# RWKV-6 and SiLU layer on one core: keys ahead of a weight sum, a tail ahead of its heads, one pair of copies on another engine, one unit's products in another order

## The chip, the core and the metric

The kernel runs on one core of a Trainium2 chip. The core has a matrix engine (TensorE, PE in the profile; its weight loads are shown apart as PEld), three engines for elementwise work (VectorE or DVE, ScalarE or ACT, GpSimd or POOL), a queue engine that issues most transfers (SyncE or SP), and 16 DMA engines. PSUM is the memory that PE writes; SBUF is the working memory. The metric is the device time of one execution in microseconds (us), as the median of three.

## What is computed

Two layers follow one another. The first is a linear recurrence over 768 time steps, for 4 batches and 8 heads of 48 channels:

```
for t in range(S):
    cur = u * k_t outer v_t
    y_t = r_t @ (state + cur)
    state = w_t[:, None] * state + k_t outer v_t
```

Its output is laid out as 3072 tokens by 384 channels, and goes through a layer of two matrix products with SiLU between them:

```
h = x @ w_in          # 384 x 2048
g = h / (1 + exp(-h))
out = g @ w_out       # 2048 x 384
```

All of it is in float32.

## The kernel before, in words

**Units.** The work is cut into 12 units of 128 time steps for two batches (6 stretches of time by 2 pairs of batches; unit i has number `i`, so the second unit is unit 1 and the third is unit 2). For a unit the recurrence is turned into products: `r` and `k` are scaled by growing products of `w`, level by level (`grow_queries` L626, `grow_keys` L632, levels 0 to 6), PE forms the scores of each level (`score_products` L691), VectorE writes them under a mask into the tile `score` (`keep_masked` L721), and PE multiplies scores and values (`x_products` L885 for units 0 and 1, `y_state` and `y_values` L840 to L876 later). The two layers behind it run one or two units late: while unit i is in its recurrence, unit i-1 is in its first product (`up` L1081 for units 0 to 2, `first_part` L1202 from unit 3 on) and unit i-2 in its second (`down` L1270 for unit 0, `quarter` L1312 after that).

**Order.** The order of all instructions is written out by hand. Each engine runs its own instructions in that order; semaphores join the engines. The early units are written out step by step (L1386 to L1442). From unit 3 on, `mix` (L967) gives groups of recurrence steps, and the loop at L1444 puts a counted number of the steps of `downs` (L1369, of unit i-2) and `ups` (L1353, of unit i-1) behind each group.

**Weights.** The 16 blocks of weights are rounded before use, each in three steps: `head_weight` (L221, two ScalarE instructions at L228 and L230), `tail_weight` (L232, one ScalarE instruction at L236 that writes the PSUM tile `p_w`), `join_weight` (L239, two VectorE instructions at L247 and L248, the second of which empties `p_w`), and `add_weight` (L256, one GpSimd addition at L260). `up(0, m)` needs block m. `join_weight` also issues the transfers of later blocks.

**Unit 1's start.** Its turned keys come from PE through four ScalarE copies (L386, L387). `odd_ones` (L659, ScalarE) and `start_keys` (L665) fill level 1's room of keys: with `own` true, two GpSimd products (L672) write the keys that the first scores of unit 1, `scores(1, 1)`, read; with `own` false two more change the rest in place. `turn_apart(0)` (L819) turns unit 0's keys back into the two PSUM banks `p_sc`, and `turn_k(0)` (L828) copies them to SBUF. `scores(1, 1)` writes the same two banks.

**Second product.** From unit 1 on `quarter` forms the second product by Winograd's seven products of half-size blocks. `sums` (L1295, VectorE, L1308) makes the four sums s1 to s4 of g, in four parts along the contraction. `quarter(i, which)` runs 16 matmuls (L1337) into one of three PSUM rooms: x, z, x, y, x, y, x for products 0 to 6. Products 2, 4 and 6 add onto what stands in x, and 5 onto y. ScalarE copies the room after 0, 2, 3 and 6 (L1342); VectorE adds after 1, 4 and 5 (L1345). Product 2 reads s2, product 3 reads s1, product 4 reads s3 and product 5 reads s4; `sums` makes them in the order s1, s3, s2, s4. For unit 2 and later, the rooms x, y, z are the banks `o0`, `o1`, `h1` that unit i+1's `first_part` uses next.

**First product.** From unit 3 on `first_part` forms h by 20 products of blocks (4x3 blocks of the weight by 3x2 of x, which the plain way takes 24 products), accumulated in four PSUM banks A to D (`ORDER` L1197), with copies, joins (L1220, VectorE) and SiLUs (L1217, ScalarE) between them. After product 1 VectorE runs two joins: one makes s32 from bank D, the other adds v22 onto bank A. Bank A is next written by product 11, three products later.

Of the kernel before, what the change touches and what calls it, by code (L numbers as in the profile page):

```python
# [15 lines left out]
ALU = mybir.AluOpType  # L16
# [22 lines left out]
def kernel(  # L39
# [11 lines left out]
    nc = tc.nc  # L51

    B, H, S, D = r.shape
# [5 lines left out]
    PD = 64  # L59
# [279 lines left out]
    for b in range(NB):  # L339
        for x in range(2):  # L340
            nc.vector.tensor_single_scalar(out=own_mask[:, b, :, x:x + 1], in_=first[0], scalar=tok[:, x, b:b + 1],
                                           op=ALU.is_equal)
# [485 lines left out]
    def turn_k(i):  # L828
        both_kq = pt.tile([128, NB, NP, 2 * PD], F32, name="kq", bufs=1)
        for b in range(NB):  # L830
            kq[i, b] = both_kq[:, b]
        for e, have in enumerate(apart[i]):
            nc.scalar.copy(out=both_kq[:, :, :, PD * e:PD * e + D], in_=have)

    p_yt, p_kv, yt = {}, {}, {}

# [124 lines left out]
    def both(fn, i, *args):  # L961
        return [(fn, i, b, *args) for b in range(NB)]
# [114 lines left out]
    FH, DH = FC // 2, DM // 2  # L1077
    NFAST = 3
# [106 lines left out]
    def first_layer(i, n):  # L1185

        place, first = ORDER[n]
        p = kept[place][:].rearrange("p (q t) -> p q t", q=4)
        left, right = left_of[n], right_of[i, n]
        for q in range(4):  # L1190
            for h in (0, PD):
                f = q * 128 + h
                nc.tensor.matmul(p[h:h + PD, q, :], lhsT=left[:, f:f + PD], rhs=right, start=first and q == 0, stop=q == 3,  # L1193
                                 skip_group_check=True)
# [7 lines left out]
    def first_part(i, n):  # L1202

        first_layer(i, n)
        pa, pb, pc, pd = (kept[x][:].rearrange("p (q t) -> p q t", q=4) for x in (A_AT, B_AT, C_AT, D_AT))

        def g(f, t):
            key = (i, PARTS[f][0], t - 1, PARTS[f][1])
            if key not in gt:
                gt[key] = pt.tile([128, 4, L], F32, name="gt", bufs=FC // 2)  # L1210
            return gt[key]

        def copy(out, in_):
            nc.scalar.copy(out=out, in_=in_)

        def silu(f, t, have):
            nc.scalar.activation(out=g(f, t), in_=have, func=AF.Silu)  # L1217

        def join(out, one, two, op):
            nc.vector.tensor_tensor(out=out, in0=one, in1=two, op=op)  # L1220

        u11, s32, s42, v22, w21 = (3, 1), (3, 2), (4, 2), (2, 2), (4, 1)
        if n == 20:
            copy(pb, pa)
        elif n == 18:
            copy(g(*u11), pc)
        elif n == 14:
            copy(g(*s32), pd)
        elif n == 13:
            join(pd, g(*u11), pa, ALU.subtract)  # L1230
        elif n == 15:
            silu(1, 1, pc)
        elif n == 4:
            copy(pc, pd)
        elif n == 7:
            nc.scalar.activation(out=g(*s42), in_=pb, func=AF.Copy, scale=-1.0)
            join(pb, pb, g(*s32), ALU.add)
        elif n == 19:
            join(g(*s42), g(*s42), pa, ALU.add)
        elif n == 16:  # L1240
            copy(g(*v22), pc)
        elif n == 1:
            join(g(*s32), g(*s32), pd, ALU.subtract)
            silu(3, 2, g(*s32))
            join(pa, pa, g(*v22), ALU.add)
        elif n == 9:
            silu(2, 2, pc)
        elif n == 11:
            copy(g(*w21), pa)
            join(pc, pb, g(*u11), ALU.subtract)  # L1250
            join(pb, pb, g(*w21), ALU.subtract)
        elif n == 6:
            silu(1, 2, pd)
        elif n == 10:
            join(pd, g(*s42), pb, ALU.add)
            silu(4, 1, pb)
        elif n == 5:
            silu(2, 1, pa)
        elif n == 8:
            silu(3, 1, pc)  # L1260
        elif n == 17:
            silu(4, 2, pd)
# [47 lines left out]
    ob, partial, sum_of = {}, {}, {}  # L1310

    def quarter(i, which):  # L1312

        n, b0 = units[i]

        def g(b, half):
            if i >= NFAST:
                return lambda f: gt[i, half, b, f // 4][:, f % 4, :]
            return lambda f: gt[i, (f + half * FH) // 2][:, f % 2, b * L:(b + 1) * L]

        def s(x):
            return lambda f: quarters[:, x, f, :]

        left, right = ((g(0, 0), b11), (g(0, 1), b21), (s(1), t2), (s(0), t1), (s(2), t3), (s(3), b22), (g(1, 1), b12))[which]
        if which == 0:
            ob[i] = [out_room(b) for b in range(NB)]
            partial[i] = pt.tile([128, 4, DH], F32, name="partial", bufs=1)
        place = "xzxyxyx"[which]
        if which in (0, 1, 3):
            if i < NFAST - 1:  # L1330
                pool, tag = (ps, "p_h") if place == "z" else (second[0], "p_o")
                sum_of[i, place] = pool.tile([128, DH], F32, name=tag, bufs=2)
            else:
                sum_of[i, place] = bank("p_sc", DH) if i == len(units) - 1 and which == 0 else kept[{"x": "o0", "y": "o1", "z": "h1"}[place]][:, 0:DH]
        p = sum_of[i, place]
        for f in range(FH):
            nc.tensor.matmul(p, lhsT=left(f), rhs=right[:, f, :], start=which in (0, 1, 3) and f == 0, stop=f == FH - 1,  # L1337
                             skip_group_check=True)
        c11, c12, c21, c22 = (ob[i][x][:, y * DH:(y + 1) * DH] for x in range(2) for y in range(2))
        u1, u2, u5 = (partial[i][:, x, :] for x in range(3))  # L1340
        if which in (0, 2, 3, 6):
            nc.scalar.copy(out={0: u1, 2: u2, 3: u5, 6: c21}[which], in_=p)  # L1342
        else:
            to, known = {1: (c11, u1), 4: (c22, u5), 5: (c12, u2)}[which]
            nc.vector.tensor_tensor(out=to, in0=p, in1=known, op=ALU.add)  # L1345
        final = i == len(units) - 1
        if which >= 5 or final and which in (1, 4):
            b = 1 if which in (4, 6) else 0
            row0 = (b0 + b) * S + n * L
            columns = slice(0, DM) if not final else slice(0, DH) if which in (1, 6) else slice(DH, DM)  # L1350
            nc.sync.dma_start(out=out[row0:row0 + L, columns], in_=ob[i][b][:, columns])
# [15 lines left out]
        return steps  # L1367

    def downs(i):  # L1369
        return [[(quarter, i, x)] for x in range(7)]  # L1370

    def do(*steps):
        for fn, *args in steps:
# [21 lines left out]
    for l in range(1, NL):  # L1395
# [1 line left out]

    do((bonus, 1, 0), (bonus, 1, 1), (product, 1, 0), (bonus, 1, 2), *both(x_products, 0), (join_weight, 0), (add_weight,),
       (x_copy, 0, 0), (tail_weight, 1), (x_copy, 0, 1), (turn_apart, 0), (turn_in, 1, 1, "k"), *both(turn, 1, "k"), (join_weight, 1),
       (odd_ones, 1), (add_weight,), (start_keys, 1, nc.gpsimd, True), (head_weight, 2), (grow_queries, 1, 0), (tail_weight, 2),  # L1400
       (up, 0, 0), (turn_k, 0), (join_weight, 2), *blocks[4:8],
       (start_keys, 1, nc.gpsimd, False), (add_weight,), (tail_weight, 3), (odd_keys, 1, 1), (head_weight, 3), (grow_keys, 1, 1),
       (scores, 1, 1, (join_weight, 3)), (add_weight,), (up, 0, 1), (tail_weight, 4), (grow_keys, 1, 2), (head_weight, 4),
# [92 lines left out]
```

## Time and profile before

| what | value |
|---|---|
| median of 3 executions | 567.58 us (567.09 to 568.59) |
| the profiled execution, its own time | 567.68 us |
| its span in the trace | 565.9 us, so 1.8 us lie around it |
| busy share of the span | PE 98%, PEld 92%, VectorE 84%, GpSimd 70%, ScalarE 48% |
| mean granted clock of PE | 0.997 |

The span runs from the first to the last instruction of the program. Busy time of PE counts overlapping pipeline time of matmuls, so 98% hides short waits; they show in the waits of PE and of its weight loads, and in the timeline. "x12" in a row is a count of instructions, the first number the start in us from the span's start, the second the length, and a note in brackets the idle time before it with what ended that idle time.

Where the stages lie: unit 1's recurrence begins near 31 us and ends near 66 us; unit 2's seven products of `quarter` run from 168.29 to 187.5 us, while unit 4's recurrence starts and unit 3's `first_part` follows from 188.81 us. Units 4 to 11 then repeat with about 42 us each.

### The profile page before, as it was taken

The page shows a single profiled execution, that of the slowest core. Times are in us where ns is not written, and L with a number is a line of the kernel's source. Part 1 is how long each engine was busy: PE and PEld are TensorE (multiplying, and loading weights), DVE is VectorE, ACT ScalarE, POOL GpSimd, SP SyncE. Part 2 cuts the span into 40 slices and gives each one's busy share as a digit, 9 for nine tenths or more (in the row PEclk, how much of TensorE's full clock was granted, in tenths as well). Part 3 has the DMA queues.
Part 4 walks back from the last instruction along what each step waited for, and adds up shares of the span by engine and source line. Part 5 has one row for each costly group of instructions (what it writes and reads, how often), then busy time and mean ns, then how long its engine had stood idle before and what let it go on. Part 6 is the DMA issues. An engine that isn't in the chain of part 4 may idle for free.

```text
span 565.9 us, 18889 instructions
## 1 busy us (share of the span) xinstructions
PE 556.3 (98%) x7782; PEld 518.0 (92%) x7782; DVE 477.0 (84%) x744; ACT 274.0 (48%) x619; POOL 397.4 (70%) x448
## 2 busy tenths in 40 slices
PE   8989999999999999999999999999999999999997
PEld 8768776699889999999999999999999999999997
DVE  7979788998999999999889989989989989882250
ACT  5679696362361373373374274274274272371330
POOL 6998988627779998969796696696696696700000
PEclk9999999999999999999999999999999999999999
DMA  9956866345445365265565554565555462102000
GB/s 223 312 109 196 208 218 125 48 67 111 108 74 98 73 112 95 57 130 96 102 105 96 109 93 88 108 97 94 111 90 94 105 99 61 38 4 57 29 9 21
DMA packets 206485, 57.59 MB, mean 102 GB/s; under 512 B 186048, under 2 KB 198208, under 8 KB 206400
## 3 DMA queue, kind: packets, MB, share of 16 engines
q1 hardware_dynamic: 203712, 54.23, 46.8%
q10 hardware_dynamic: 2688, 2.16, 1.6%
q8 instruction: 61, 1.00, 0.8%
q14 instruction: 24, 0.20, 0.1%
HBM read 47.14 MB, written 9.18 MB: 100 GB/s over the span
## 4 chain that ended last, share of the span: by engine, by line
PE 71%; DVE 11%; DMA 5%; POOL 5%; issue 3%; SPq 3%; ACT 0%; DVEq 0%; POOLq 0%
PE p_o L1337 24%; PE p_o L1193 14%; PE p_h L1193 9%; PE p_h L1086 5%; PE p_m L1275 4%; PE p_h L1337 4%; PE p_sc L706 3%; DVE temps L1308 2%; PE p_sc L1337 2%; PE p_m L870 2%; DVE tr L629 2%; DVE score L724 2%; PE p_m L849 1%; POOL tk L647 1%; DMA tokens_w<-in_w_dram 1%
## 5 line engine op out<-in xcount | busy, mean ns | idle before, releaser
L647 POOL TENSOR_TENSOR tk<-tk,tw 128x256 f32<-128x256 f32 x112 | 92.4, 845 | 5.1 <-PE p_sc L706 1.5
L1337 PE MATMUL p_o<-own,temps 128*128 128x192 f32 x496 | 82.9, 326 | 0.7 <-DVE temps L1308 0.7
L1337 PEld LDWEIGHTS p_o<-own,temps 128*128 128x128 f32 x496 | 80.8, 190 | 1.0 <-DVE temps L1308 0.9
L1193 PE MATMUL p_o<-xt,w_in_sb 128*64 128x128 f32 x1152 | 72.1, 273 | 0.0
L416 POOL TENSOR_TENSOR tw<-tw 128x256 f32<-128x256 f32 (+6 forms) x71 | 42.3, 595 | 37.5 <-DVE tw L366 34.0
L1086 PE MATMUL p_h<-xt,w_in_sb 128*128 128x256 f32 x288 | 67.8, 391 | 0.7 <-POOL w_in_sb L260 0.7
L1193 PEld LDWEIGHTS p_o<-xt,w_in_sb 128*64 128x64 f32 x1152 | 64.7, 137 | 0.1
L1086 PEld LDWEIGHTS p_h<-xt,w_in_sb 128*128 128x128 f32 x288 | 54.7, 194 | 9.4 <-POOL w_in_sb L260 1.1
L498 POOL TENSOR_TENSOR ruk<-tokens_rk 128x384 f32<-128x384 f32 x48 | 54.2, 1148 | 9.4 <-DMA tokens_rk<-in_k_dram 9.4
L1337 PE MATMUL p_o<-w_out_sb,gt 128*128 128x192 f32 x308 | 54.5, 330 | 0.4 <-DVE ob L1345 0.3
L629 DVE TENSOR_TENSOR tr<-tr,tw 128x512 f32<-128x512 f32 x57 | 51.0, 895 | 1.1 <-PE p_m L706 0.4
L1337 PEld LDWEIGHTS p_o<-w_out_sb,gt 128*128 128x128 f32 x308 | 50.0, 190 | 1.6 <-DVE ob L1345 1.0
L1308 DVE TENSOR_TENSOR temps<-gt 128x512 f32<-128x512 f32 (+1 forms) x48 | 43.7, 947 | 0.0
L656 POOL TENSOR_TENSOR tk<-tk,tw 128x256 f32<-128x256 f32 x32 | 25.1, 815 | 26.5 <-DVE tk L366 26.5
L1342 ACT COPY partial<-p_o 128x192 f32<-128x192 f32 x31 | 9.9, 319 | 67.3 <-PE p_o L1337 59.7
L617 ACT COPY tk<-tk 128x256 f32<-128x256 f32 x52 | 20.9, 401 | 38.2 <-POOL tk L647 27.4
L1217 ACT ACTIVATE gt<-p_o 128x512 f32<-128x512 f32 x45 | 26.0, 601 | 25.0 <-PE p_o L1193 25.0
L1337 PE MATMUL p_o<-w_out_sb,temps 128*128 128x192 f32 x176 | 30.5, 327 | 0.1
L724 DVE COPY_PREDICATED score<-mask,p_sc 128x512 f32<-128x512 int8 x38 | 28.4, 804 | 1.4 <-PE p_sc L706 1.3
L1337 PEld LDWEIGHTS p_o<-w_out_sb,temps 128*128 128x128 f32 x176 | 28.8, 190 | 0.4 <-ACT partial L1342 0.4
L1337 PE MATMUL p_h<-w_out_sb,gt 128*128 128x192 f32 x168 | 29.1, 326 | 0.0
L498 POOL TENSOR_TENSOR spare<-tokens_rk 128x384 f32<-128x384 f32 x24 | 28.4, 1197 | 0.6
(255 smaller groups left out, 1313.4 us busy)
## 6 DMA issues: line engine op xcount, KB each, us to landing
w_out_sb<-in_moe_w_in_dram SPq DMA_DIRECT2D x6, 768.0 KB, 7.2
turned<-yt SPq DMA_DIRECT2D x18, 192.0 KB, 2.6
xt<-turned SPq DMA_DIRECT2D x9, 384.0 KB, 3.4
w_out_sb<-in_moe_w_out_dram SPq DMA_DIRECT2D x4, 768.0 KB, 7.0
own<-in_moe_w_out_dram SPq DMA_DIRECT2D x4, 768.0 KB, 4.4
tokens_w<-in_w_dram SPq DMA_DIRECT2D x8, 384.0 KB, 4.4
tokens_rk<-in_r_dram SPq DMA_DIRECT2D x7, 384.0 KB, 4.3
tokens_rk<-in_k_dram SPq DMA_DIRECT2D x7, 384.0 KB, 5.9
```

The source lines that it names most:

```text
L416: engine.tensor_tensor(out=up, in0=t[:, :, 0::2], in1=t[:, :, 1::2], op=ALU.mult)
L498: mul = lambda out, one, two: nc.gpsimd.tensor_tensor(out=out, in0=one, in1=two, op=ALU.mult)
L629: nc.vector.tensor_tensor(out=odd, in0=odd, in1=tw[i][l][:, :, 0::2][:, :, :, None].to_broadcast([128, Q, L >> (l + 1), c]), op=ALU.mult)
L647: nc.gpsimd.tensor_tensor(out=out, in0=have, in1=odd_products(i, l, b, *blocks), op=ALU.mult)
L656: nc.gpsimd.tensor_tensor(out=have, in0=have, in1=odd_products(i, l, b, [2, NP * ni]), op=ALU.mult)
L724: nc.vector.copy_predicated(out=dst, mask=masks[l][:, :, None].to_broadcast([128, NB, NP, ni, c]), data=sc[e].rearrange("p (b q) (i c) -> ...
L1086: nc.tensor.matmul(p_h[:, a, :], lhsT=w_in_sb[:, c, f * 128:(f + 1) * 128], rhs=xt[i][:, c, :], start=(a == 0 and c == 0), stop=(a == 1 an ...
L1193: nc.tensor.matmul(p[h:h + PD, q, :], lhsT=left[:, f:f + PD], rhs=right, start=first and q == 0, stop=q == 3, skip_group_check=True)
L1217: nc.scalar.activation(out=g(f, t), in_=have, func=AF.Silu)
L1275: nc.tensor.matmul(po[i, b], lhsT=gt[i, f // 2][:, f % 2, b * L:(b + 1) * L], rhs=w_out_sb[:, f, :], start=(f == 0), stop=(f == FC - 1))
L1308: nc.vector.tensor_tensor(out=out, in0=one, in1=two, op=op)
L1337: nc.tensor.matmul(p, lhsT=left(f), rhs=right[:, f, :], start=which in (0, 1, 3) and f == 0, stop=f == FH - 1, skip_group_check=True)
```

## The change

It touches five places. Nothing of the arithmetic changes but the place and order of some additions.

- `turn_k` of unit 0: its two copies out of PSUM run on VectorE and no longer on ScalarE.
- `first_part`, product 1: the join that adds v22 onto bank A stands ahead of the join for s32 and the SiLU behind it (all units from 3 on).
- `quarter` of unit 2 (`i == NFAST - 1`): product 6 starts afresh in room z. For that, ScalarE also copies room x after product 4 (to a fourth part of `partial`, u3), and VectorE adds u3 to product 6's copy: one more instruction on each.
- `downs` of unit 2: the products run in the order 0, 1, 3, 2, 5, 4, 6.
- The order written out for unit 1's start: the two own-key products stand ahead of the addition of weight block 1 on GpSimd, and the tail of block 2 ahead of its two heads on ScalarE.

```diff
@@ turn_k
         for e, have in enumerate(apart[i]):
-            nc.scalar.copy(out=both_kq[:, :, :, PD * e:PD * e + D], in_=have)
+            (nc.scalar.copy if i else nc.vector.tensor_copy)(out=both_kq[:, :, :, PD * e:PD * e + D], in_=have)
@@ first_part
         elif n == 1:
+            join(pa, pa, g(*v22), ALU.add)
             join(g(*s32), g(*s32), pd, ALU.subtract)
             silu(3, 2, g(*s32))
-            join(pa, pa, g(*v22), ALU.add)
@@ quarter
-        place = "xzxyxyx"[which]
-        if which in (0, 1, 3):
+        apart_6 = i == NFAST - 1
+        place = ("xzxyxyz" if apart_6 else "xzxyxyx")[which]
+        fresh = (0, 1, 3, 6) if apart_6 else (0, 1, 3)
+        if which in fresh:
...
-            nc.tensor.matmul(p, lhsT=left(f), rhs=right[:, f, :], start=which in (0, 1, 3) and f == 0, stop=f == FH - 1,
+            nc.tensor.matmul(p, lhsT=left(f), rhs=right[:, f, :], start=which in fresh and f == 0, stop=f == FH - 1,
                              skip_group_check=True)
...
-        u1, u2, u5 = (partial[i][:, x, :] for x in range(3))
-        if which in (0, 2, 3, 6):
-            nc.scalar.copy(out={0: u1, 2: u2, 3: u5, 6: c21}[which], in_=p)
-        else:
-            to, known = {1: (c11, u1), 4: (c22, u5), 5: (c12, u2)}[which]
-            nc.vector.tensor_tensor(out=to, in0=p, in1=known, op=ALU.add)
+        u1, u2, u5, u3 = (partial[i][:, x, :] for x in range(4))
+        if which in (0, 2, 3) or which == 6 or which == 4 and apart_6:
+            nc.scalar.copy(out={0: u1, 2: u2, 3: u5, 4: u3, 6: c21}[which], in_=p)
+        if which in (1, 4, 5) or which == 6 and apart_6:
+            to, known = {1: (c11, u1), 4: (c22, u5), 5: (c12, u2), 6: (c21, u3)}[which]
+            nc.vector.tensor_tensor(out=to, in0=to if which == 6 else p, in1=known, op=ALU.add)
@@ downs
-        return [[(quarter, i, x)] for x in range(7)]
+        return [[(quarter, i, x)] for x in ((0, 1, 3, 2, 5, 4, 6) if i == NFAST - 1 else range(7))]
@@ the order of unit 1's start
-       (odd_ones, 1), (add_weight,), (start_keys, 1, nc.gpsimd, True), (head_weight, 2), (grow_queries, 1, 0), (tail_weight, 2),
+       (odd_ones, 1), (start_keys, 1, nc.gpsimd, True), (add_weight,), (tail_weight, 2), (head_weight, 2), (grow_queries, 1, 0),
        (up, 0, 0), (turn_k, 0), (join_weight, 2), *blocks[4:8],
```

## The prediction

> **What bounds the kernel now.** I read the waits of PE and of its weight loads first, because PE is busy 98% of the span: a change can gain only where PE waits, runs at a lower clock, or has another chain beside it that is as long.
>
> ```profile
> PE p_sc L706 <- POOL tk L672: 1.6, 1, 1.6
> ...
> PE p_o L1337 <- DVE temps L1308: 0.7, 1, 0.7
> ```
>
> ```profile
> PEld p_o L1337 <- DVE temps L1308: 0.9, 1, 0.9
> ...
> PEld p_h L1193 <- DVE p_h L1220: 0.8, 2, 0.4
> ```
>
> The columns are total us, times, longest. The change aims at these: the first scores of unit 1 wait 1.6 us for the own keys (L672), one product of unit 2 waits 0.9 us for a sum, and product 11 of `first_part` waits twice, 0.4 us each, for the join on bank A. From 31 us on no other single wait of either is longer than 0.9 us. Next, the table by windows, for the clock (the number behind the five busy times):
>
> ```profile
> 12.50:15.90 3.40, 2.34 (x26) 1.76 (x24) 3.29 (x6) 0.45 (x2) 2.49 (x4) 1.00 1.13 211
> ...
> 36.40:39.80 3.40, 1.94 (x37) 1.66 (x38) 2.76 (x3) 2.57 (x6) 2.74 (x5) 1.00 0.41 51
> 39.80:43.20 3.40, 3.40 (x10) 2.66 (x9) 3.30 (x4) 2.50 (x5) 3.05 (x4) 0.50 0.84 242
> ```
>
> The stretch that holds the 1.58 us wait has PE busy for 1.94 of 3.40 us (57%), and the next runs at clock 0.50: `up(0, 1)`'s 12 matmuls take 4.47 us and not 2.86. A stretch at 2.34 (69%) was not followed by a lower clock. The timeline from 33 to 45 us shows who made PE wait:
>
> ```profile
> 33.52 0.69 DVE L629 TENSOR_TENSOR tr<-tr,tw 128x512 f32<-128x512 f32 x1
> ...
> 33.68 2.20 POOL L260 TENSOR_TENSOR w_in_sb<-temps 128x768 uint32<-128x768 uint32 x1 [0.35 <-DVE temps L248]
> ...
> 35.85 2.53 POOL L672 TENSOR_TENSOR tk<-tk,tw 128x128 f32<-128x128 f32 x4
> 35.99 0.85 ACT L236 ACTIVATE p_w<-w_out_sb 128x768 f32<-128x768 uint16 x1
> ...
> 36.87 0.96 DVE L247 SCALAR_TENSOR_TENSOR p_w<-w_out_sb,p_w 128x768 uint32<-128x768 uint32 x1 [2.67 <-ACT p_w L236]
> ...
> 43.34 0.60 ACT L1095 ACTIVATE own<-p_h 128x512 f32<-128x512 f32 x1 [0.62 <-PE p_h L1086]
> ...
> 44.74 0.96 DVE L247 SCALAR_TENSOR_TENSOR p_w<-own,p_w 128x768 uint32<-128x768 uint32 x1 [0.78 <-ACT p_w L236]
> ```
>
> The own keys stand behind block 1's addition (33.68 to 35.88), and VectorE idles 2.67 us for block 2's tail. From 44.74 on VectorE has no idle over 0.14 us until 66 us, and GpSimd, behind it, ends block 7's addition at 63.03; `up(0, 7)` starts at 63.08. So past 44 us this chain, not PE alone, sets when PE reaches 63 us. After that PE runs through to 141 us. The chain of waits around unit 2's products is:
>
> ```profile
> 150.90 7.14 DMA tokens_w<-in_w_dram
> ...
> 166.04 1.84 DMA raw<-in_r_dram
> 167.90 1.30 DVE tk L366 x2
> ...
> 174.70 1.73 DVE temps L1308 x3
> 176.43 0.04 issue
> 176.47 11.32 PE p_o L1337 x68
> ```
>
> It leads from PE at 141 us over VectorE's reductions and SP into transfers, to VectorE, and back to PE. From 188 us a second such loop (PE, VectorE, block-sum transfers, VectorE, PE) runs to 272 us; behind it PE has no waits of size to the end.
>
> **Part 1, unit 1's start (order and `turn_k`).** I replay it from the rows.
> - Own keys: the turned keys are done at 33.51 (last L387), GpSimd is free at 33.33. Two products by 0.66 us. They now stand beside `grow_queries` (33.52 to 34.21); in unit 2 an L672 beside an L629 took 1.15 and its neighbours 0.67, so 0.47 more. End: 33.5 + 1.32 + 0.47 = 35.3 (before 37.13).
> - Copies of `turn_k` on VectorE: two by 0.56 (VectorE's copy of 128x384 out of PSUM, L905), from 34.2 to 35.3, inside the 2.67 us idle time. They free the `p_sc` banks; ScalarE did so at 38.10. Without that idle time they would cost 1.1 us. VectorE's PSUM copies at L940 (two by 0.55) stood beside an L260 of 1.82 us, so I charge GpSimd nothing for them.
> - Scores: PE is free at 36.2 and starts them there and not at 37.82: 1.6 us less.
> - Block 1's addition: 35.3 + 1.83 (an L260 that no L629 overlaps) = 37.1, 1.25 us later than before. `up(0, 1)` waits for it and starts at 37.15 (before 38.78). PE's wait shrinks to about 0.35 us, the stretch is over 80% busy, so by the rows the clock stays at 1.00.
> - Tail 2 follows `odd_ones` on ScalarE: 34.2 to 35.1 (before 36.84). Join 2: 35.3 to 37.3 (before 38.90). The heads end at 37.0, before block 2's addition needs them. That addition stands behind the two other key products: 37.1 + 1.3 + 1.83 = 40.2 (before 40.88).
> - From there the chain: level 1's two key products 1.45 (41.7), ScalarE's copy 0.42, SiLU 0.60, tail 4 0.87, so join 4 starts at 43.4 to 43.5 and not at 44.74. That is 1.25 us less. If the own keys meet less of `grow_queries` than I charged, 1.65. If they must also wait for `odd_ones` (34.25), 0.9. The three key products that wait for ScalarE do so for three different instructions, of which `odd_ones` would be the last, so I take 1.4.
>
> The rest of the early stage hangs on VectorE and moves with it. SP gets no new transfer; block 8's, issued in join 2, stands behind SP's own queue until 40.03 as before. So **PE passes 63 us 1.4 us earlier**, not 1.6 plus the 1.7 us that half clock cost: those are beside the chain.
>
> The Trainium skill, "SBUF — State Buffer", section "Who interferes with whom", speaks against this reorder: a VectorE instruction with two SBUF inputs and a GpSimd instruction that reads SBUF lock each other out, and the later one fully waits. By it the own keys would lose the whole 0.66 us left of `grow_queries` and not 0.47, and the sum would be 0.2 us smaller. The row (1.15 against 0.67) shows less, and I use it.
>
> **Part 2, unit 2's products.** Product 2 stood 0.95 us for the last part of s2, done at 176.43. In the new order product 3 is there, and reads s1, done by 175.3 (first of the L1308 at 174.70); its last quarter is due at 175.5, so no stall. Product 2 then needs s2 at 178.1, products 5 and 4 need s4 and s3, done by 176.88. ScalarE's copies (0.32) between products into the same room have a product between them. PE gains 0.92 us up to the scores at 187.72; their second half needs `prepare` (L785, done 186.99), which is early enough. Product 6 in z needs bank `h1` emptied (the add at 180.85) and must itself be copied before product 20: the scores between (0.96 us) cover that copy (0.32); without them it would cost 0.5 us. Room x is now freed by product 4's add, which stands where product 5's stood (189.67), for product 14 that would start at 189.65: 0.1 us. What follows:
>
> ```profile
> 192.69 0.70 DVE L1220 TENSOR_TENSOR p_o<-gt,p_h 128x512 f32<-128x512 f32 x1 [0.95 <-PE p_h L1193]
> ```
>
> This join opens the second loop. It waits 0.95 us for PE, VectorE being free at 191.74. The new add of u3 (0.35, as L1345; no row shows it with both inputs in SBUF, between nothing and L1308's 0.43 for 256 columns) pushes that to 192.1. So the loop opens **0.6 us earlier**; bounds 0 and 0.92.
>
> **Part 3, the join on bank A.** It may save the two waits (0.44 at 200.2, 0.39 at 244.0). Both lie inside the second loop, where PE waits again for VectorE (0.56 at 228.3, 0.44 at 271.6), so I take 0; bounds 0 and 0.8. The s32 join moves back by 0.7 us; product 3 needs its bank 2.6 us after product 1.
>
> **Sum.** 1.4 + 0.6 + 0 = 2.0 us off the profiled execution's 567.68 (span 565.9 and 1.8 around it): 565.7; this execution stood 0.1 above the median of 567.58, so **565.6 us** as a median. The bounds (0.9 + 0 to 1.65 + 0.92 + 0.8) give 564.2 to 566.7.
>
> **Rivals.**
> - *PE is the bound throughout*: the waits and the half clock all count: 1.6 + 1.7 + 0.9 = 4.2, 563.4 us. For it: PE runs without gaps from 38.8 to 62.9. Against: additions end just ahead of `up` (54.26 for 54.50, 63.03 for 63.08).
>   The Trainium skill, "TensorE: Matmul & The Clock Gate", "What's actually happening", has the clock fall only after at least one idle window of some 3.4 us; by that rule a 1.58 us wait didn't cause it and its end doesn't cure it, and this rival falls to 565.1. Here the fall followed a stretch that was 57% busy.
> - *Only one part arrives*: block 1's later addition holds the early chain, or the second loop is opened by GpSimd and not by this join: 566.2 (part 1 alone) to 567.0 (part 2 alone).
> - *A strip lands late, and it ends slower*: at 166.04 a strip of `raw` took 1.84 us to land and released VectorE's turn of k. Strips take 1.7 to 6.6 us. If the earlier PE work moves this one among other transfers and it takes 6.6, the loop loses 4.8: 570.4 us. It decides from a landing 2 us later than now. Against: all that feeds SP's queue there starts from VectorE at 147.5 and moves along.
>
> **Chances.** About 0.3% (1.7 us) is what a measurement of this kernel can tell from no change, so the line to faster is 565.9. The forecast has 0.60, of which three quarters lie under that line; PE throughout 0.15; one part alone 0.12; the late strip 0.13. Faster 0.45 + 0.15 = 0.60, same 0.15 + 0.12 = 0.27, slower 0.13. The range, 563.3 to 567.4, leaves out the late strip and the edges.
>
> **What would show it.** Right: L672 starts near 33.5 and ends near 35.3; no wait of PE on it; clock 1.00 from 39.8 to 43.2; join 4 near 43.4; `up(0, 7)` near 61.7; unit 2's products without a gap; the L1220 of 192.69 near 190.7. Wrong: half clock stays or appears elsewhere; join 4 moves but `up(0, 7)` doesn't; the `raw` strip or the block sums land at their old times.

## The result, and the profile after

| | before | after |
|---|---|---|
| median | 567.14 us (566.55 to 568.59, 11 runs) | 566.15 us (565.31 to 567.39, 11 runs) |
| profiled execution: time, span | 567.68, 565.9 us | 566.43, 564.6 us |
| mean granted clock in it | 0.997 | 1.0 |

The ratio of after to before is **0.9976 (95% interval 0.9967 to 0.9986)**, 1.4 us less (the two medians, taken by themselves, differ by 1.0 us). The gain is clear of zero, but it is under the 0.3% at which the prediction drew the line to "faster"; it had given that side of the line 0.60. Run again beside other kernels, the changed kernel gave 0.9982 (0.9969 to 0.9995). The forecast was 2.0 us.

**Unit 1's start came as forecast.** The timeline of the changed kernel from 33 to 45 us (start us, us, engine, line, operation):

```profile
33.34 1.75 POOL L672 TENSOR_TENSOR tk<-tk,tw 128x128 f32<-128x128 f32 x2
...
33.57 1.00 DVE L629 TENSOR_TENSOR tr<-tr,tw 128x512 f32<-128x512 f32 x1
...
34.48 1.01 DVE L833 COPY kq<-p_sc 128x384 f32<-128x384 f32 x2
...
36.23 0.70 PE L706 MATMUL p_sc<-tr,tk 48*64 48x64 f32 x32
...
43.06 0.96 DVE L247 SCALAR_TENSOR_TENSOR p_w<-own,p_w 128x768 uint32<-128x768 uint32 x1 [0.61 <-ACT p_w L236]
```

The own keys end at 35.09, the copies of `turn_k` at 35.49, the scores start at 36.23 without a wait, and join 4 starts at 43.06, 1.68 us earlier than before. The same two stretches of the table by windows (the number behind the five busy times is the clock):

```profile
36.40:39.80 3.40, 3.39 (x44) 2.59 (x40) 3.33 (x4) 3.32 (x6) 3.40 (x4) 1.00 0.42 51
39.80:43.20 3.40, 3.21 (x41) 2.62 (x44) 2.69 (x5) 2.51 (x5) 3.40 (x5) 1.00 0.51 99
```

PE is busy through the first and keeps its full clock in the second. What PE waits for in the early stage now are the weights' additions, as these lines of the waits of PE's weight loads and of PE show (total us, times, longest):

```profile
PEld p_h L1086 <- POOL w_in_sb L260: 3.0, 6, 0.9
...
PE p_h L1086 <- POOL w_in_sb L260: 1.5, 3, 0.7
```

So the chain of heads, tails, joins and additions sets the pace there, as the prediction had it. `up(0, 7)` starts at 61.55 and not 63.08. Set against the first `up` of unit 0, which stood 0.05 us later in this execution, PE has gained **1.58 us** at 63 us.

**Unit 2's products did not.** The gap at 176 us is gone: at 190 us PE is 2.52 us ahead of before, 0.96 more than at 174. Then the timeline from 187 us shows this:

```profile
188.07 0.89 DVE L1347 TENSOR_TENSOR ob<-ob,partial 128x192 f32<-128x192 f32 x1
188.70 2.09 POOL L498 TENSOR_TENSOR ruk<-tokens_rk 128x384 f32<-128x384 f32 x2
...
190.94 0.69 DVE L1220 TENSOR_TENSOR p_o<-gt,p_h 128x512 f32<-128x512 f32 x1
...
197.88 1.09 PE L1193 MATMUL p_o<-xt,w_in_sb 128*64 128x128 f32 x16 [0.73 <-POOL w_in_sb L1132]
```

The new addition of u3 took 0.89 us and not 0.35. The join L1220 does start 1.75 us earlier and no longer waits for PE. But PE then waits at product 9 for GpSimd's weight sum q9, 0.73 us for the product and 0.97 for its weight load. PE is 1.50 us ahead at 205, 1.12 at 210, and 1.25 from 275 us to the end: all that the new order of products had won is gone within 15 us, and some of part 1's gain with it. The chain of waits of the changed kernel says who holds PE there:

```profile
164.42 1.93 DMA raw<-in_r_dram
166.36 0.72 DVE tk L366
...
168.98 1.42 POOL w_in_sb L1132
...
188.74 2.05 POOL ruk L498 x2
190.79 2.48 POOL w_in_sb L1132 x2
...
193.34 2.97 POOL w_in_sb L1132 x2
196.53 1.26 issue
197.79 1.67 POOL tk L647 x2
```

From 167 to 199 us it hardly leaves GpSimd, which has no gap over 0.1 us there; it starts from the strip of `raw` that lands at 166.35. In the kernel before, the chain there went through PE's products. GpSimd's queue from 167 to 190 us moved by 1.55 us, as the strip's landing did (1.53), and not by PE's 2.5.

### The profile page after: what moved, and what is told of

Same layout as the page of the kernel before. It is cut to its first block, busy times and chain, and to the rows that moved or that the text cites. A ratio compares the mean times of both kernels' runs of the same rounds, so it can differ in the third digit from the quotient of the medians.

```text
span 564.6 us, 18890 instructions
## 1 busy us (share of the span) xinstructions
PE 555.2 (98%) x7782; PEld 516.8 (92%) x7782; DVE 477.3 (85%) x747; ACT 272.0 (48%) x618; POOL 396.2 (70%) x448
## 4 chain that ended last, share of the span: by engine, by line
PE 68%; POOL 12%; DVE 8%; DMA 4%; issue 3%; SPq 3%; ACT 1%; DVEq 0%; POOLq 0%
PE p_o L1339 22%; PE p_o L1193 13%; PE p_h L1193 9%; PE p_h L1086 4%; PE p_m L1275 4%; PE p_h L1339 4%; POOL tk L647 2%; PE p_sc L706 2%; PE p_sc L1339 2%; SPq L127 2%; POOL ruk L498 2%; PE p_m L870 2%; POOL tw L416 2%; POOL w_in_sb L1132 2%; DVE tr L629 2%
## 5 line engine op out<-in xcount | busy, mean ns | idle before, releaser
L647 POOL TENSOR_TENSOR tk<-tk,tw 128x256 f32<-128x256 f32 x112 | 88.6, 811 | 5.1 <-PE p_sc L706 1.5
L416 POOL TENSOR_TENSOR tw<-tw 128x256 f32<-128x256 f32 (+6 forms) x71 | 42.3, 595 | 38.2 <-DVE tw L366 34.8
L1086 PE MATMUL p_h<-xt,w_in_sb 128*128 128x256 f32 x288 | 66.3, 384 | 1.8 <-POOL w_in_sb L260 1.5
L1086 PEld LDWEIGHTS p_h<-xt,w_in_sb 128*128 128x128 f32 x288 | 53.5, 190 | 10.4 <-POOL w_in_sb L260 3.0
L498 POOL TENSOR_TENSOR ruk<-tokens_rk 128x384 f32<-128x384 f32 x48 | 54.3, 1152 | 9.3 <-DMA tokens_rk<-in_k_dram 9.3
L629 DVE TENSOR_TENSOR tr<-tr,tw 128x512 f32<-128x512 f32 x57 | 53.4, 937 | 1.1 <-PE p_m L706 0.4
L1339 PE MATMUL p_o<-w_out_sb,gt 128*128 128x192 f32 x292 | 51.7, 330 | 0.3 <-DVE ob L1347 0.3
L1339 PEld LDWEIGHTS p_o<-w_out_sb,gt 128*128 128x128 f32 x292 | 47.4, 190 | 1.5 <-DVE ob L1347 0.9
L656 POOL TENSOR_TENSOR tk<-tk,tw 128x256 f32<-128x256 f32 x32 | 25.1, 813 | 27.2 <-DVE tk L366 22.6
L1308 DVE TENSOR_TENSOR temps<-gt 128x512 f32<-128x512 f32 (+1 forms) x48 | 43.7, 948 | 0.0
L1339 PE MATMUL p_h<-w_out_sb,gt 128*128 128x192 f32 x184 | 31.9, 326 | 0.0
L1339 PEld LDWEIGHTS p_h<-w_out_sb,gt 128*128 128x128 f32 x184 | 30.2, 190 | 0.0
```

The source lines that it names most:

```text
L416: engine.tensor_tensor(out=up, in0=t[:, :, 0::2], in1=t[:, :, 1::2], op=ALU.mult)
L498: mul = lambda out, one, two: nc.gpsimd.tensor_tensor(out=out, in0=one, in1=two, op=ALU.mult)
L629: nc.vector.tensor_tensor(out=odd, in0=odd, in1=tw[i][l][:, :, 0::2][:, :, :, None].to_broadcast([128, Q, L >> (l + 1), c]), op=ALU.mult)
L647: nc.gpsimd.tensor_tensor(out=out, in0=have, in1=odd_products(i, l, b, *blocks), op=ALU.mult)
L656: nc.gpsimd.tensor_tensor(out=have, in0=have, in1=odd_products(i, l, b, [2, NP * ni]), op=ALU.mult)
L1086: nc.tensor.matmul(p_h[:, a, :], lhsT=w_in_sb[:, c, f * 128:(f + 1) * 128], rhs=xt[i][:, c, :], start=(a == 0 and c == 0), stop=(a == 1 an ...
```

## Experiments

"Ahead" is how much earlier PE starts the same matmul than in the profiled execution of before. Where several profiles are compared, the early stage is measured from the first `up` of unit 0 (33.38 us), which stands up to 0.9 us later or earlier from one of these executions to the next, but for the one with the idle transposes, where it stood 8.9 us later.

### Part 1 alone

```diff
@@ turn_k
-            nc.scalar.copy(out=both_kq[...], in_=have)
+            (nc.scalar.copy if i else nc.vector.tensor_copy)(out=both_kq[...], in_=have)
@@ order of unit 1's start
-  (add_weight,), (start_keys, 1, nc.gpsimd, True), (head_weight, 2), (grow_queries, 1, 0), (tail_weight, 2),
+  (start_keys, 1, nc.gpsimd, True), (add_weight,), (tail_weight, 2), (head_weight, 2), (grow_queries, 1, 0),
```

> The kernel before with part 1 alone (own keys ahead of the addition, tail ahead of heads, copies on VectorE). Theory A (part 2's gain on PE is taken back by GpSimd's weight sums and by VectorE's slow add, so part 1 carries the whole gain): PE is 1.5 us earlier at 63 us and at 188 us, still 1.2 to 1.6 us earlier at 290 us, and the time is 0.997 to 0.998 of before, the same as the whole change. Rival B (the parts add up, and the loss behind 188 us would hit part 1 as well): 1.5 us at 188 us shrink to 0.6 to 0.9 at 290 us, and the ratio is 0.9985 to 0.999.

Measured: 565.43 us median (564.98 to 565.92), ratio 0.9966 (0.9954 to 0.9978). PE is ahead by 1.58 us at 63 us from the first `up`, as in the whole change; without that correction it is ahead by 1.20 there and by 2.24 at the end. Part 1 carries all of the gain, and alone it is no worse than the whole. But there was a surprise: between 174 and 190 us PE gained another 0.82 us with the old order of products. The wait at which part 2 aims was not there.

### Part 2 alone, and parts 1 and 3

The first has only the hunks of `quarter` and `downs`; the second is the kernel of part 1 with

```diff
@@ first_part, product 1
+            join(pa, pa, g(*v22), ALU.add)
             join(g(*s32), g(*s32), pd, ALU.subtract)
             silu(3, 2, g(*s32))
-            join(pa, pa, g(*v22), ALU.add)
```

> The kernel before with part 2 alone (unit 2's products reordered, product 6 in room z). Theory A: PE is unmoved at 63 us, 0.95 us earlier at 188 us, loses all of it between 196 and 210 us to a wait for a weight sum of GpSimd (L1132) and to the slow add on VectorE, and ends 0 to 0.3 us later or earlier: ratio 0.9995 to 1.0005. Rival B: 0.6 us earlier to the end, ratio 0.999.

Measured: 567.40 us median (566.63 to 573.56), ratio 1.001 (0.9991 to 1.0029): no gain. Its profiled execution alone would have misled: it had a span of 564.9 us, 1.0 below before's. In it PE won 0.96 us from 174 to 190 us and had half of that lost again at 210, but ended 1.0 us ahead, which fits neither theory. The section on the strip of k comes back to it.

> Parts 1 and 3 without part 2. Theory A: as part 1 alone; the two waits for the join on bank A (0.4 us each) go, but PE waits as long elsewhere before 275 us, so no more than 0.2 us better than part 1 alone: ratio 0.997 to 0.998. Rival B: the whole change is better than this by 0.6 us. Rival C (the join's waits count at the end): 0.4 to 0.8 us better than part 1 alone.

Measured: 565.96 us median, ratio 0.9969 (0.9956 to 0.9981), the same as part 1 alone (0.9966). Again the wait at 176 us was not there, without the new order. Part 3 takes away the 0.4 us wait for bank A in the profile and nothing at the end.

### The half clock

```diff
-       (up, 0, 0), (turn_k, 0), (join_weight, 2), *blocks[4:8],
+       (up, 0, 0), (beat, 6), (beat, 6), (turn_k, 0), (join_weight, 2), *blocks[4:8],
```

The kernel before, with twelve idle transposes on PE ahead of the scores that waited.

> The kernel before with 12 transposes of the unit matrix, whose result nobody reads, put on PE ahead of unit 1's first scores, where it waits 1.58 us. If low business of PE causes the half clock, the stretch from 39.8 to 43.2 us runs at 1.00. Theory A (the chain over SiLU, tail 4 and join 4 sets the pace): join 4 starts 0.4 us earlier and PE is 0.4 us earlier at 63 us. Rival D (PE sets the pace): 1.7 us earlier at 63 us. If the clock is half all the same, the cause is not PE's business as counted in the rows.

Measured: ratio 0.9993 (0.9978 to 1.0009). 1.7 us would be 0.997, outside the interval, but that does not price the half clock: 18 of the 24 runs of before in this comparison had a mean clock of 0.999 or 1.0 and no such stretch to cure. The profiled execution had PE at half clock from 13.9 to 27.5 us, ahead of the stretch in question. Behind its first `up` the clock stayed at 1.00, and PE was 0.18 us ahead at 63 us, nearer to Theory A's 0.4 than to Rival D's 1.7; one execution that began so differently is weak evidence.

The runs of the kernel before in the three comparisons say it better. Of 77, 57 had a mean clock of 0.9985 or more, with a median of 567.41 us, and 17 had 0.996 to 0.998, which is what one stretch of 3.4 us at half clock makes of 566 (the profiled one had such a stretch and 0.997), with a median of **567.50**. (The other three had 0.990 to 0.994 and 569.9 to 570.65 us.) The medians are 0.1 us apart and the means 0.5, so the 1.7 us that PE loses in such a stretch are worth far less than 1.7 at the end. A run's mean clock doesn't tell where its stretch lies, so the exact price stays open.

### The strip of k, and parts 1 and 2

Why was the wait at 176 us gone without the reorder? The waits of GpSimd differ. The lines are from 150 to 200 us; first the kernel before, then part 1 alone:

```profile
POOL ruk L498 <- DMA tokens_rk<-in_k_dram: 4.0, 1, 4.0
```

```profile
POOL ruk L498 <- DMA tokens_rk<-in_k_dram: 2.6, 1, 2.6
```

A transfer of 384 KB, a strip of k (`tokens_rk`), took 6.6 us from issue to landing in the changed kernel, in which GpSimd waited 4.0 us for it as in the one before, and 5.2 or 5.3 in these four experiments. GpSimd then starts L498 1.4 us sooner against VectorE's sums (L1308), and its work (L498 and the L416 behind it) stands beside fewer of them. Such a sum takes 0.42 us alone and 1.1 to 1.3 beside that work. The sixth sum is the one that differs: 1.26 us in before and 0.41 in part 1 alone. VectorE gains 0.8 us, and s2 is there when product 2 wants it.

```diff
@@ parts 1 and 2: the changed kernel, but in first_part
-            join(pa, pa, g(*v22), ALU.add)
             join(g(*s32), g(*s32), pd, ALU.subtract)
             silu(3, 2, g(*s32))
+            join(pa, pa, g(*v22), ALU.add)
```

> Parts 1 and 2 without part 3 (the two joins behind product 1 in their old order). Two explanations stand for the 0.95 us wait for s2 at 176 us, at which part 2 aims. Theory E, 'the strip': the wait is there only where the 384 KB strip of k lands in 6.6 us (the kernels before and after as profiled; GpSimd then waits 4.0 us for it), and not where it lands in 5.2 (parts 1, 2, and 1 with 3, alone; GpSimd waits 2.5 to 2.6 us): GpSimd's L498 then stands beside fewer of VectorE's sums, and VectorE gains 0.8 us by itself. By it part 2 adds nothing to part 1, and takes 0.1 to 0.5 us by its longer addition: ratio to before 0.9966 to 0.9975, near 565.6 us, and if the strip lands early, PE's gain between 174 and 190 us is about 0.8 us as with part 1 alone. Rival F, 'the reorder': part 2's 0.95 us are its own and come on top of part 1: ratio 0.995, near 564.5 us, and PE's gain between 174 and 190 us is 0.9 us wherever the strip lands, with 0.8 more on VectorE. Without part 3 the 0.4 us waits for the join on bank A should be back; by my prediction they cost nothing at the end.

Measured: 566.64 us median (565.62 to 569.97), ratio 0.9985 (0.9969 to 1.0001). This time the strip took 6.6 us. PE was ahead by 0.54 us at 174, 1.50 at 190, and 0.46 at 205: the reorder's 0.96 us won, then as much lost at product 9, with a wait of 0.74 us like the 0.73 of the changed kernel. The ratio lies above Theory E's 0.9966 to 0.9975, whose upper part is inside the interval; Rival F's 0.995 is outside. Rival F has the local gain right and its end wrong.

### What carries part 1: the copies or the own keys?

```diff
@@ the changed kernel, but in turn_k
-            (nc.scalar.copy if i else nc.vector.tensor_copy)(out=both_kq[...], in_=have)
+            nc.scalar.copy(out=both_kq[...], in_=have)
```

> The changed kernel, but with the turned k of unit 1 copied by ScalarE as before; order and products as changed. Theory G, 'the copies': in the kernel before, the scores of unit 1 were held not by the own keys (done at 37.13) but by ScalarE's two copies (37.25 to 38.10), which free the banks; so here the own keys end near 35.1 and PE still waits, until about 37.5, some 1.3 us; the clock may fall behind it; PE gains only what the earlier tail and joins give, 0.2 to 0.5 us at 63 us, ratio 0.9985 to 1.000. Rival H, 'the own keys', as the waits of before name them: the scores start at 36.3 and PE gains 1.5 us at 63 us, ratio 0.9976.

Measured: ratio 1.0003 (0.9986 to 1.002). The timeline of this kernel:

```profile
33.04 1.74 POOL L672 TENSOR_TENSOR tk<-tk,tw 128x128 f32<-128x128 f32 x2
...
36.99 0.85 ACT L833 COPY kq<-p_sc 128x384 f32<-128x384 f32 x2
37.56 1.03 PE L706 MATMUL p_sc<-tr,tk 48*64 48x64 f32 x32 [1.57 <-POOL tk L672]
```

The own keys are done at 34.78, yet PE waits until 37.56, and the profile still names L672. The last thing to end ahead of the scores is the first of ScalarE's two copies (36.99 to 37.46), which empties a bank that they need. At 63 us PE is ahead by 0.02 us, measured from the first `up`: nothing at all, under Theory G's 0.2 to 0.5. The clock stayed at 1.00, though this wait is as long as before's 1.58.

```diff
@@ the kernel before, but in turn_k
-            nc.scalar.copy(out=both_kq[...], in_=have)
+            (nc.scalar.copy if i else nc.vector.tensor_copy)(out=both_kq[...], in_=have)
```

> The kernel before, with nothing changed but the turned k of unit 1 copied by VectorE. Theory G: the banks are free at 35.5, the own keys end at 37.1, so the scores start at 37.2 and not 37.8, PE waits 0.9 us and not 1.6; block 1's addition still ends at 35.9, so the chain of tails and joins does not move, except where it waited for PE: gain at 63 us 0 to 0.6 us, ratio 0.999 to 1.000. Rival H: the scores wait for the second own key at 37.13 to 37.8 as before, no gain at all, and ScalarE's freed 0.9 us brings tail 2 forward from 36.0 to 35.1, with the joins behind it: gain at 63 us 0.9 us. Neither alone gives the 1.55 us of part 1 by Theory G.

Measured: 567.05 us median (566.55 to 568.13), ratio 0.9984 (0.9971 to 0.9998). Its timeline:

```profile
34.80 1.01 DVE L833 COPY kq<-p_sc 128x384 f32<-128x384 f32 x2
...
36.52 2.54 POOL L672 TENSOR_TENSOR tk<-tk,tw 128x128 f32<-128x128 f32 x4
...
37.86 0.70 PE L706 MATMUL p_sc<-tr,tk 48*64 48x64 f32 x32 [0.93 <-POOL tk L672]
```

Now the own keys are the last. The scores start 0.65 us earlier, measured from the first `up`, and 0.22 us are left at 63 us. So the order alone gives 0.02, the copies alone 0.22, and both 1.58: each takes away one of two releasers that end 0.6 us apart in before (own keys 37.13, first copy 37.72). The lead at 63 us can be seen earlier in GpSimd's additions: the one of block 3 ends at 45.65 in before, 45.66 with the order alone, 45.46 with the copies alone and 44.08 with both (measured from the first `up`). Theory G holds for what the scores wait for, though its 0.2 to 0.5 us for the order alone did not come; Rival H falls in both runs. In this profile the strip took 7.0 us, and the wait at 176 us was back (0.63 us).

### The addition of u3 from its bank

```diff
@@ the changed kernel, but in quarter
-        if which in (0, 2, 3) or which == 6 or which == 4 and apart_6:
+        if which in (0, 2, 3) or which == 6 and not apart_6 or which == 4 and apart_6:
...
-            nc.vector.tensor_tensor(out=to, in0=to if which == 6 else p, in1=known, op=ALU.add)
+            nc.vector.tensor_tensor(out=to, in0=p, in1=known, op=ALU.add)
```

> The changed kernel, but product 6 of unit 2 is added from its bank (VectorE, one input in PSUM) and not copied to SBUF by ScalarE and then added (both inputs in SBUF). In the changed kernel that addition took 0.88 us beside GpSimd's L498 where I had put 0.35. If the two SBUF inputs beside GpSimd are the reason, it takes 0.3 to 0.45 us here, and the first sum behind it (L1220 of 190.94 in the changed kernel) moves 0.5 us earlier; L498 beside it takes 1.00 and not 1.12. At the end: my theory, that GpSimd's weight sums and not this addition set when PE goes on at 197 us, expects 0 to 0.3 us (ratio 0.9972 to 0.9976); the rival, that the addition is what lost part 2's gain, expects 0.5 us or more (0.9967 or less). If the strip of k lands early here, the wait for the weight sum at 197 us should be 0.2 us or less and not 1.0.

Measured: 566.99 us median (565.63 to 569.67), ratio 0.9992 (0.9975 to 1.0009), a result that neither theory gave. Its timeline:

```profile
188.30 0.34 DVE L1347 TENSOR_TENSOR ob<-p_h,partial 128x192 f32<-128x192 f32 x1
...
188.70 1.09 PE L1193 MATMUL p_h<-gt,in_sum 128*64 128x128 f32 x16 [1.28 <-DVE ob L1347]
```

The size is settled: with one input in PSUM the addition takes 0.34 us, with both in SBUF it took 0.89, both beside an L498 that started 0.38 us ahead of it. The next L498 takes 1.01 and not 1.12, but here the addition was over before it began. VectorE's next instruction follows 0.55 us sooner. But the bank that product 6 used is what unit 3's first product needs. ScalarE's copy had emptied it early; now PE waits 1.28 us for VectorE, and the join L1220 comes at 192.52 and not 0.5 us ahead of 190.94. Neither theory had asked who frees the bank. Four of the twelve runs had a mean clock of 0.996 or 0.997 and a median of 568.72 us, the other eight 566.25; whether the low clock comes from this wait is not shown, since the profiled execution had 1.00.

### Part 1 and the whole change side by side

> Part 1 alone, once more, beside the whole change on the same chip. Theory J: part 2 gives nothing wherever the strip of k lands. If it lands early (GpSimd waits 2.6 us for it), PE has no wait for s2 at 176 us even with the old order of products; if it lands late (4.0 us), PE waits 0.6 to 0.9 us here and the gain of part 1 stays at 1.5 us from there to the end. Ratio to before 0.9963 to 0.9978; ahead of the whole change by 0 to 0.8 us. Rival K (part 2 does pay, and part 1 alone was lucky in its runs): behind the whole change by 0.3 us or more.

> The changed kernel, once more, beside part 1 alone. Theory J: ratio to before 0.997 to 0.9985; if the strip lands late, PE gains 0.95 us at 176 us and loses 0.9 to 1.0 of it at 197 us to the weight sum of product 9 (a wait of 0.7 us or more there); if early, GpSimd is 0.5 us further ahead and that wait is 0.2 us or less, but PE has nothing of part 2's own to lose. Rival K: ratio 0.9965 or less, ahead of part 1 alone.

Measured on the same chip: part 1 alone 565.99 us (565.23 to 566.58), ratio 0.9970 (0.9958 to 0.9981); the whole change 566.59 (565.51 to 567.88), ratio 0.9982 (0.9969 to 0.9995). Part 1 alone has the lower median here by 0.6 us, and in the first runs by 0.7, but the intervals of the ratios overlap both times. It is not shown to be better, only to be no worse. The waits from 150 to 200 us, first part 1 alone, then the whole change:

```profile
POOL ruk L498 <- DMA tokens_rk<-in_k_dram: 3.8, 1, 3.8
PEld p_o L1337 <- DVE temps L1308: 0.9, 1, 0.9
PE p_o L1337 <- DVE temps L1308: 0.6, 1, 0.6
```

```profile
POOL ruk L498 <- DMA tokens_rk<-in_k_dram: 2.7, 1, 2.7
PEld p_o L1193 <- POOL w_in_sb L1132: 0.3, 1, 0.3
```

The strip came late for the first (6.4 us) and early for the second (5.3), and Theory J's waits are there: with the old order and a late strip the wait for s2; with the new order and an early strip only 0.3 us for q9 (0.2 or less expected). Over all profiles this makes a table. It shows how PE's lead changes from 166 us to the end (minus is a gain):

| | strip of k late (GpSimd waits 3.8 to 4.3 us) | early (2.5 to 2.7 us) |
|---|---|---|
| old order of products | 0 (before, by definition), +0.04 (copies only), -0.09 (part 1 again) | -1.01 (part 1), -0.63 (parts 1 and 3) |
| new order | +0.31 (after), +0.47 (parts 1 and 2) | -0.90 (part 2), -0.55 (copies stay), -0.70 (after again) |

(The runs with the direct addition and without q8 are not in it, nor is the one with the idle transposes, an old order with an early strip: -0.95.) Between late and early lie 0.5 to 1.4 us whatever the order. Each cell has two or three profiles, and no run set the landing, so this goes with the strip but isn't an experiment on it. Within a column the new order is on average slower, by about 0.4 us with a late strip and about 0.1 with an early one; the second is within the scatter.

### Without one weight sum

```diff
-  (8, nc.gpsimd, ("q8", "q1", "q5", "q9")),
+  (8, nc.gpsimd, ("q1", "q5", "q9")),
```

> The changed kernel without the weight sum q8 (one GpSimd addition of 1.28 us ahead of product 9's; product 8 of unit 3 then uses a quarter of the weights as loaded, so that part of the result is another). Theory J: the wait at 197 us, and only the late GpSimd, took back part 2's gain: with q9 due 1.3 us earlier the wait for it goes, and PE keeps what it has at 190 us, to within 0.15 us, through 200 us. With a late strip that is 0.95 us more than the changed kernel keeps there; at the end 0.5 to 1.0 us less than the changed kernel, ratio 0.995 to 0.9965. Rival L, 'VectorE anyway': the gain would have been lost a few us later to VectorE's joins or scores, whatever GpSimd does: no wait for q9, but PE waits 0.5 us or more between 198 and 211 us, and the end is within 0.3 us of the changed kernel.

Measured: 564.76 us median (564.38 to 565.69), ratio 0.9953 (0.9941 to 0.9965). The strip was early (5.3 us). There was no wait for q9, and PE kept its 0.96 us from 174 to 190 us past 200. The end came as Theory J had it, and more: 1.8 us under the change of the same comparison. But PE then waited 1.07 us at 205.7 us, as Rival L said, although the end was not the one that it gave:

```profile
202.72 0.01 DVE L568 LOAD_MASK_SELECT spare<-spare  x1 [0.92 <-DMA spare<-kept]
...
203.00 1.98 DVE L574 COPY_PREDICATED score<-late_masks,spare 128x1024 f32<-128x1024 int8 x1
204.88 0.69 DVE L1220 TENSOR_TENSOR p_o<-gt,p_h 128x512 f32<-128x512 f32 x1
...
205.71 1.09 PE L1193 MATMUL p_o<-xt,w_in_sb 128*64 128x128 f32 x16 [1.07 <-DVE p_o L1220]
```

PE waits there for a join that stands behind VectorE's masks, and VectorE had itself waited 0.92 us for the block sums' transfer (`spare<-kept`). So with q9 out of the way, something else holds PE.

> Part 1 alone, without the weight sum q8 (left out as in the run before). Theory J: with the old order of products, PE stands behind the sums, and q9 never holds it; so q8's 1.28 us on GpSimd are hidden, and the end is within 0.3 us of part 1 alone. The difference between the two kernels without q8 is then what part 2 is worth where GpSimd does not take it back: 0.95 us at 200 us if the strip lands late, 0.1 us if early. Rival L: GpSimd's 1.28 us are on the path here too (scores and sums behind 200 us wait for it), 0.5 us or more at the end.

Measured: 564.79 us median (564.41 to 567.51), ratio 0.9960 (0.9945 to 0.9975), 1.2 us under part 1 alone. Theory J had expected 0.3 at most, so it fails here and Rival L holds, as far as these two medians go (the intervals overlap): GpSimd's 1.28 us are on the path with the old order too. The strip was late and the wait for s2 was there (0.67 us), so PE had no more room at 190 us than before; the gain came later. GpSimd, 1.3 to 2.7 us further ahead from 194 us on, let go of VectorE's sums sooner: one L1308 at 215 us took 0.69 and not 1.41, and PE's lead grew by 0.7 us between 220 and 230 us (0.6 had come by 205). And the two kernels without q8 end alike (564.76 and 564.79): with GpSimd out of the way the new order of products is still worth nothing that these runs can tell.

## Why the prediction was off by 0.6 us, point by point

**Part 1: right, and a little larger.** Predicted 1.4 (0.9 to 1.65) at 63 us; measured 1.57 to 1.60 in all nine profiles that hold the whole of part 1. The prediction named the own keys as what held the scores, as the waits do; the copies alone and the order alone show that ScalarE's first copy held them last. Since both were moved, the sum did not suffer. The steps came within 0.4 us: own keys' end 35.3 (35.09), scores 36.2 (36.23), `up(0, 1)` 37.15 (36.94), join 4 at 43.4 (43.06), `up(0, 7)` 61.7 (61.55). The contention was shared and not one-sided. The own keys took 1.75 us and not 1.32, and `grow_queries` beside them 1.00 and not 0.69. The Trainium skill, "SBUF — State Buffer", section "Who interferes with whom", has such pairs shut each other out. By the prediction's reading one of them waits fully; here both lost a part, 0.43 and 0.31 us.

In three of those nine profiles 0.4 to 0.6 us were lost again at 85 us, where PE's scores waited for VectorE's `grow_queries`. The chain leads back to a transfer each time, but not to the same one. In the run of parts 1 and 2 it is a block of the weights (`w_out_sb<-in_moe_w_out_dram`, landing at 80.3 us), which held ScalarE's rounding for 0.6 us. With the direct addition it is an earlier block (`own<-in_moe_w_out_dram`, landing at 70.5 us) and a strip of `raw` behind it. In the second run of the change it is a strip of k (landing at 66.1 us), and a `grow_queries` of 1.12 and not 0.76 us is added. I had not looked that far: "The rest of the early stage hangs on VectorE and moves with it" has exceptions.

**Part 2: the step that failed** is "This join opens the second loop", which the prediction sized at 0.6 us. Its working was right as far as PE: 0.92 predicted, 0.96 measured. The new addition was mis-sized (0.35 against 0.89 us, at bounds of 0 to 0.43 taken from rows with PSUM inputs or no L498 beside them). Yet the addition did not decide: the join opened 1.75 us earlier and the gain was lost all the same. GpSimd's queue did, in the two profiles with the new order and a late strip, where PE lost 0.95 us at product 9. It is full from 167 to 199 us, it starts from a strip that part 2 does not move, and product 9's weights stand at its end. Taking 1.28 us out of it gained 1.2 to 1.8 us at the end. But it is not the only holder: without q8 the two orders of products end alike, and PE with the new order waits for VectorE instead. So the step that failed is shown, and that GpSimd takes the gain first; how much each later holder would take is not. The prediction had this as a rival, in the words "the second loop is opened by GpSimd and not by this join", with 566.2 us as its time and a chance shared with another case at 0.12. The gain by the ratio, 1.4 us, is the one of that rival. That the median itself (566.15) comes so close is in part luck, since before's median came out 0.44 us below the 567.58 that the prediction started from. The sign stood in the trace of before:

```profile
197.81 1.28 POOL L1132 TENSOR_TENSOR w_in_sb<-w_in_sb,in_sum 128x512 f32<-128x512 f32 x1
...
199.38 1.04 PE L1193 MATMUL p_o<-xt,w_in_sb 128*64 128x128 f32 x16
```

The first line is q9, which ended at 199.09 us; GpSimd had no idle time over 0.1 us on the way there from 169; the second is product 9. So PE had 0.3 us to move up there, not 0.92. I had followed only the PE and VectorE pieces of the chain.

**Part 2 was also aimed at a wait that not every execution has.** I took the 0.95 us from one profile and priced it as if it stood in all. It was there in every profile that had the old order and a late strip (four of four), and in none with an early strip (three of three, but for a weight load's 0.2 us in the one with the idle transposes).

**Part 3: right.** Predicted 0; part 1 with it and without it gave 0.9969 and 0.9966.

**PE the bound throughout: wrong**, as the low chance said. The half clock in the early stage is worth little at the end (0.1 us by the medians, 0.5 by the means). With the order alone and with the copies alone the clock stayed at 1.00 there, and PE had still only 0.02 and 0.22 us at 63 us: the additions ahead of `up` set its pace.

**A late strip of raw: wrong strip.** It landed in 1.93 us (before 1.84). But the mechanism was real for other transfers: the strip of k at 150 us and those behind the loss at 85 us.

**The sum** is then: 1.58 in part 1, less some 0.2 on average for the loss at 85 us (0.4 to 0.6 in three of nine), less 0.1 to 0.4 for the new products, makes 1.0 to 1.3 us. Measured were 1.4 and 1.0. The lowest ratios of kernels that leave no work out are those of part 1 alone (0.9966 and 0.9970, so 1.9 and 1.7 us), 0.3 to 0.6 us more gain than the same sum without the new products; how often the strip lands late in either kernel is not known, and no run settles that rest. What stays open is why the strip of k takes 5.3 or 6.6 us in the same program; no run here changed how it is issued.

## What to carry to other kernels

Before a wait is priced, look at the queues of the engines that PE meets next: one that has no idle time between the wait and the next meeting, and does not move with the wait, will take the gain back. When two releasers end close together, the profile names one of them, and removing either alone gains next to nothing; look for the second in the timeline before sizing the gain. And a wait behind a transfer should be seen in more than one execution before a change is built on it.

## What the hardware showed that I had not expected

- A stretch of PE at half clock followed a wait of 1.5 to 1.6 us in the profiles of before and of part 2 alone, and did not in that of the kernel whose copies stayed on ScalarE (1.57 us). Among the runs of before, the mean clock fits one such stretch in 17 of 77. The Trainium skill, "TensorE: Matmul & The Clock Gate", section "What's actually happening", says that the window in which activity is judged runs freely. By that the same program can fall on either side, and the counts agree. It also says that the clock falls after at least one idle window of some 3.4 us; here it fell behind a wait of half that.
- A VectorE addition with both inputs in SBUF took 0.89 us beside GpSimd's L498, and 0.34 beside the same L498 with one input in PSUM.
- The same 384 KB transfer, issued at the same place of the program, took 5.2 or 5.3 us in eight profiles and 6.4 to 7.0 in five others, and the end differs with it by 0.5 to 1.4 us: as much as the whole change gives.
